# Attention, gated layer and soft mixture on one core: the token sum in feature halves, a second score bank, five raw buffers, and whole loads and stores at the end

## The chip, the cores and the metric

The kernel runs on one core of one Trainium2 chip. The metric is the device time of one execution, in microseconds (us). TensorE (PE) multiplies, VectorE (DVE), ScalarE (ACT) and GpSimd (POOL) work on elements, and SyncE (SP) issues every DMA of this kernel, in one queue and in program order.

## The reference

```python
scores = scale * np.matmul(q, k.transpose(0, 1, 3, 2))      # q, k, v: 4 x 12 heads x 448 x 64
scores = np.where(mask, -1e9, scores)                       # causal
attn = softmax(scores); x = (attn @ v) -> 1792 tokens x 768
h = x @ w_in                                                # 768 -> 2048, weights given as float64
g = h * clip(h + 3, 0, 6) / 6
x = g @ w_out                                               # 2048 -> 768, weights given as float64
logits = x @ phi                                            # 32 slots: 8 experts x 4
d = softmax(logits, over tokens);  slot_input = d.T @ x     # 32 x 768
h = maximum(slot_input[e] @ w1[e], 0); slot_out[e] = h @ w2[e]
c = softmax(logits, over slots);   return c @ slot_out      # 1792 x 768
```

The first gated layer is the bulk of the arithmetic. Since w_out is applied to all tokens only through phi and through the token sum d.T @ g, the kernel never forms g @ w_out: it forms w_out @ phi once, and U = d.T @ g (32 x 2048) with a running maximum over the four batches.

## The kernel before, in words

**Front.** Attention runs over 24 pairs of heads, six for each of four batches (function `attention`). A pair loads q, k, v, forms scores once for the row maxima (L476), takes the maxima on DVE (L491 or L495), forms the scores again transposed and in split float32r with the maximum subtracted (L526, L531), exponentiates (L541), multiplies with v (L564) and writes its columns of x (`xp`). Two PSUM banks as one tile `ps` hold scores; two single banks `t` hold transposes. Beside it `conv` turns the float64 weights into float32 (load into a `raw` buffer, of which there are three; ACT L627; DVE L630, L636, L639): 16 tiles of w_out first, then 16 tiles of w_in.

**The gated layer.** For each batch and each of 16 feature tiles `hmm` (L734) makes 18 matmuls of 128x448. ACT adds three and clips (`r`, L739), DVE multiplies (`g`, L741). In batch 0 w_in comes from `conv`; later batches reload it from DRAM (`wi_d`, into `cx`). Logits are gathered in one bank by L767.

**Sums of a batch.** The logits of the four column groups are added by one matmul (L809); DVE takes the maximum (L866, for the last batch L827), ACT the exponential. `ublocks` (L785) then makes 56 tiled matmuls into four banks. DVE adds the four banks into `U4`, four planes of 2048 values a partition's worth (L910, L857). After the last batch eight rounds fold `U` and `U4` (L1045, L1049, with the scale held in a buffer of pool `g`), copy to `wp` (L1054) and multiply with w_out (L1062) to the slot input.

**The mixture.** 64 loads of 768 KB bring w1 and w2 into ring buffers of 6 KB a partition. Memory for rings comes free in stages, since pools close one after the other: `cv_end`, `a_end`, `b_end`, `x_end` (after the last `cx`), `h_end` (after the last L734), `g_end` (pool of `g`, `r`, `ls`, `zT`), `m_end` (`gtok`), `o_end` (after the last L1062, five more buffers in w_out's place). `RINGS` tells how many buffers each gives: 1 at the start, then 4, 2, 3, 1, 6, 2, 3. Experts run in L1109 to L1133; then L1215 multiplies with w2. For the last two experts w2 comes in column halves, so that the chain to the outputs of columns 0 to 383 (L1230 to L1238, L1255, copies L1263/L1267, eight stores of 112 partitions) may run before the second half has landed.

**What sets the order.** `Schedule` is a list scheduler that runs while the program is built. Each step has a priority number (a due time from the table `TU`), a cost and its buffers; it is put on its engine when the planner's clock says that it can start. Where the planner sees PE idle, `filler` (L390) puts in 32x128 matmuls whose result is not used. What the engines then do is fixed, in that order.

## Time and profile before

| | us |
|---|---|
| median of 3 runs (654.37 to 656.09) | 655.76 |
| the profiled execution, its own time | 655.37 |
| its span, first to last instruction | 653.5 |
| PE busy in the span | 594.8 |
| DVE busy | 407.5 |
| ACT busy | 250.4 |
| POOL busy | 150.6 |

Fillers count as busy PE. Times in the rows are from the span's start. A chain of waits tells what released each piece of work; a table by windows tells how busy each engine was in a stretch, the granted clock of PE as a share of full speed (1.00 is 2.4 GHz, 0.50 is 1.2), the busy share of the 16 DMA engines and what they moved.

### The profile page before, as it was taken

The numbers are of one execution on the slowest core, as the hardware profiler recorded it, in microseconds if no ns is written. First come the engines' busy times: TensorE is split into PE (matmuls) and PEld (weight loads), VectorE is DVE, ScalarE is ACT, GpSimd is POOL, SyncE is SP. The second block draws the span as 40 slices with busy tenths as digits, with TensorE's granted clock in tenths as the row PEclk, the third lists the DMA queues.
The fourth block names the chain that finished last, engine by engine and source line by source line (L and its number), as shares of the span: only waits on it lengthen the run. The fifth ranks groups of instructions, "written<-read, shape, count | busy, mean of one in ns | idle before, by whom it ended". The sixth has DMA issues, their size and how long they took to land.

```text
span 653.5 us, 14639 instructions
## 1 busy us (share of the span) xinstructions
PE 594.8 (91%) x5816; PEld 446.1 (68%) x5816; DVE 407.5 (62%) x948; ACT 250.4 (38%) x420; POOL 150.6 (23%) x212
## 2 busy tenths in 40 slices
PE   7799899988988889999999999999999999998582
PEld 5688676766877678758878777888788654463021
DVE  6889888679886796787686867555655423010032
ACT  2466556445455554524344541433333201110032
POOL 1234446424462222323234322210000010000000
PEclk8899999899998999999999999999999999879877
DMA  7998878879879789872676543279833449999987
GB/s 205 314 294 254 217 213 207 189 168 241 171 199 252 171 194 249 219 168 76 121 164 125 135 91 79 73 206 402 314 97 97 174 175 416 415 414 414 393 291 252
DMA packets 196244, 144.59 MB, mean 221 GB/s; under 512 B 154704, under 2 KB 174672, under 8 KB 196176
## 3 DMA queue, kind: packets, MB, share of 16 engines
q1 hardware_dynamic: 196176, 143.66, 74.5%
q8 instruction: 46, 0.75, 0.5%
q14 instruction: 22, 0.18, 0.1%
HBM read 121.41 MB, written 22.22 MB: 220 GB/s over the span
## 4 chain that ended last, share of the span: by engine, by line
PE 45%; DMA 12%; DVE 10%; SPq 2%; ACT 2%; issue 2%; DVEq 0%; ACTq 0%
PE ph L734 25%; DMA ring<-in_moe_w_dram 8%; DMA raw<-in_moe_w_in_dram 3%; DVE ps L491 3%; PE ps L526 2%; SPq L406 2%; PE t L1124 2%; PE o L564 2%; PE pl L767 1%; PE t L785 1%; PE ps L1109 1%; PE pl L734 1%; PE ph L1109 1%; PE ps L476 1%; PE o L1062 1%
## 5 line engine op out<-in xcount | busy, mean ns | idle before, releaser
L734 PE MATMUL ph<-xp,wpl 128*128 128x448 f32 x1098 | 238.3, 372 | 2.4 <-DVE wpl L723 2.3
L734 PEld LDWEIGHTS ph<-xp,wpl 128*128 128x128 f32 x1098 | 204.0, 189 | 32.7 <-issue 8.7
L739 ACT ACTIVATE r<-ph,three 128x448 f32<-128x448 f32 x61 | 38.6, 632 | 124.0 <-PE ph L734 119.3
L549 POOL TENSOR_SCALAR_AFFINE_SELECT s<-s 128x256 f32<-128x256 f32 x96 | 49.6, 540 | 145.4 <-ACT s L541 140.1
L741 DVE SCALAR_TENSOR_TENSOR g<-r,ph 128x448 f32<-128x448 f32 x61 | 37.5, 614 | 55.4 <-ACT r L739 52.4
L491 DVE CUSTOM_DVE_ANT_0 ps<-ps,maskw 128x448 f32<-128x448 f32 (+3 forms) x144 | 61.7, 428 | 15.1 <-PE ps L476 10.5
L725 POOL TENSOR_TENSOR wpl<-cx,wpl 128x768 fp32r<-128x768 f32 x26 | 49.8, 1916 | 80.7 <-ACT wpl L720 74.8
L720 ACT ACTIVATE wpl<-cx 128x768 fp32r<-128x768 f32 x64 | 53.6, 838 | 29.6 <-PE ph L734 16.0
L526 PE MATMUL ps<-qp,kp 64*64 64x64 f32 (+3 forms) x576 | 58.2, 309 | 6.7 <-DVE mc L491 2.7
L541 ACT ACTIVATE s<-ps 128x896 f32<-128x896 f32 (+2 forms) x72 | 50.0, 731 | 28.6 <-PE ps L531 25.8
L526 PEld LDWEIGHTS ps<-qp,kp 64*128 64x128 f32 (+1 forms) x576 | 42.4, 177 | 22.5 <-ACT s L541 5.1
L564 PE MATMUL o<-vr,s 128*64 128x65 f32 (+1 forms) x1536 | 53.6, 224 | 0.0
L564 PEld LDWEIGHTS o<-vr,s 128*64 128x64 f32 (+1 forms) x1536 | 48.6, 137 | 5.0 <-issue 2.9
L627 ACT ACTIVATE ca<-raw 128x768 f32<-128x768 f32 x32 | 29.4, 919 | 46.8 <-DMA raw<-in_moe_w_in_dram 26.3
L723 DVE TENSOR_TENSOR wpl<-cx,wpl 128x768 fp32r<-128x768 f32 x38 | 35.8, 943 | 3.9 <-ACT wpl L720 3.6
L476 PE MATMUL ps<-kp,qp 64*128 64x448 f32 (+1 forms) x192 | 27.3, 342 | 11.5 <-DVE mc L495 4.0
L745 DVE STREAM_TRANSPOSE gtok<-g 128x448 f32<-128x448 f32 x48 | 29.7, 632 | 4.0 <-PE ps L785 3.1
L636 DVE SCALAR_TENSOR_TENSOR cw<-ca,cw 128x768 uint32<-128x768 uint32 x32 | 30.7, 958 | 2.2 <-ACT ca L627 0.7
L476 PEld LDWEIGHTS ps<-kp,qp 64*128 64x128 f32 x192 | 14.4, 173 | 23.9 <-issue 10.1
L630 DVE TENSOR_SCALAR cw<-raw 128x768 uint32<-128x768 uint32 x30 | 18.7, 622 | 19.0 <-DMA raw<-in_moe_w_in_dram 11.1
L531 PE MATMUL ps<-dg,oner 64*128 64x448 f32 (+1 forms) x192 | 28.4, 295 | 0.0
L1215 PE MATMUL o<-ring,wos 128*32 128x384 f32 x108 | 21.3, 627 | 5.7 <-DMA ring<-in_moe_w_dram 5.7
(236 smaller groups left out, 802.0 us busy)
## 6 DMA issues: line engine op xcount, KB each, us to landing
ring<-in_moe_w_dram SPq DMA_DIRECT2D x54, 768.0 KB, 14.6
cx<-wi_d SPq DMA_DIRECT2D x48, 384.0 KB, 3.5
raw<-in_moe_w_out_dram SPq DMA_DIRECT2D x16, 768.0 KB, 6.4
raw<-in_moe_w_in_dram SPq DMA_DIRECT2D x16, 768.0 KB, 6.9
wos<-in_moe_w_dram SPq DMA_DIRECT2D x10, 768.0 KB, 15.1
wo_d<-gtok SPq DMA_DIRECT2D x16, 384.0 KB, 3.5
wi_d<-cx SPq DMA_DIRECT2D x16, 384.0 KB, 3.8
wos<-wo_d SPq DMA_DIRECT2D x16, 384.0 KB, 5.9
```

Source lines behind the costliest of these rows:

```text
L476: nc.tensor.matmul(ps.t[:n, h, c:c + w], pl["q"].t[r, 0, q0:q0 + n], pl["k"].t[r, 0, 0:w], start=(t == part[0][0]), stop=adds, skip_group_ ...
L491: nc.vector.tensor_tensor_reduce(out=x, in0=x, in1=maskw[:n, 320 - q0:320 + n] if t else maskw[:n, 320:320 + n], scale=-1.0, scalar=3.0e38 ...
L526: nc.tensor.matmul(ps.t[:kn, h, col:col + n], pl["k"].t[r, x, q0:q0 + kn], pl["q"].t[r, y, q0:S], start=(c == 0 and col == 0), stop=False, ...
L541: nc.scalar.activation(out=o, in_=x, func=ACTF.Exp, scale=SCALE)
L549: nc.gpsimd.affine_select(out=x, in_=x, pattern=[[0, 2], [1, kn]], compare_op=ALU.is_ge, fill=0.0, base=0, channel_multiplier=-1)
L564: nc.tensor.matmul(o.t[64 * h:64 * h + 64, VD * j:VD * j + VD], s.t[:kn, h, c:c + 64], vr.t[:kn, h, t, :], start=(t == 0), stop=(t == ts[- ...
L720: e = sc.add("ACT", 0.84, lambda w=w, cx=cx: nc.scalar.activation(out=w.t[:, 0], in_=cx.t, func=ACTF.Copy), [cr], [cx, w], ps_)
L723: ("DVE", 1.0, lambda w=w, cx=cx: nc.vector.tensor_sub(w.t[:, 1], cx.t, w.t[:, 0].bitcast(F32))),
L725: ("POOL", 2.0, lambda w=w, cx=cx: nc.gpsimd.tensor_sub(w.t[:, 1], cx.t, w.t[:, 0].bitcast(F32))),
L734: nc.tensor.matmul(h.t[:, :S], w.t[:, a, kk, :], x.t[:, c, kk, :], start=(n == 0), stop=(n == len(seq) - 1))
L739: rr = sc.add("ACT", 0.63, lambda h=h, r=r: nc.scalar.activation(out=r.t, in_=h.t[:, :S], func=ACTF.Relu, bias=three), [hh], [h, r], pr - ...
L741: gg = sc.add("DVE", 0.62, lambda h=h, r=r, g=g: nc.vector.scalar_tensor_tensor(out=g.t, in0=r.t, scalar=6.0, in1=h.t[:, :S], op0=ALU.min, ...
```

## The change

It has four visible parts and a new order. (1) `U4` is gone: `collect` copies the four banks of `ublocks` to SBUF (in `gtok`'s memory), adds them with four column-tiled matmuls and folds them into one `U`; after the last batch this is done in two halves of eight feature tiles, `U` is turned by DVE into `wp`, and w_out is multiplied from there without the eight rounds. `U` of batch 0 is brought into the same layout by four transposes. `r` is gone (ACT writes into `g`, DVE multiplies in place). Logits go to tokens by four DVE block transposes straight from the bank (`logits_out`), without ACT copy and PE transposes. (2) When the last user of `t` is done, its two banks become a second `ps` tile. (3) Five `raw` buffers instead of three; rings now come as 0, 6, 2, 4, 1, 5, 2, 3. (4) All w2 loads are whole; after the last one both column halves are finished, and outputs are stored by seven stores of 128 partitions, with 14 tokens of the output to a partition and two of them (6 KB) in a store. (5) The table and the planner's costs are other numbers, and the planner adds a cost where PE changes between full-array and tiled matmuls (`TURN`, `KEEP`).

```diff
-TU = {'PO': [-130.96, ...], ..., 'RINGS': [1, 4, 2, 3, 1, 6, 2, 3], ..., 'RAW': 3, ...}
+TU = {'KEEP': 2.63, 'PO': [-133.04, ...], ..., 'RINGS': [0, 6, 2, 4, 1, 5, 2, 3], ..., 'RAW': 5, ...}
...
-    U4 = const.tile([P, KF, 4, 32], F32, name="U4")
...
-        many(mog, TU["R"], "r", [P, S])
...
-        ptt = many(pst, 2, "t", [P, 512])
+        ptt = pst.tile([P, 2, 512], F32, name="pt")
+        sc.pool("t", [ptt[:, 0], ptt[:, 1]])
...
+            def collect(banks, bufs, um, up, c0, n, deps, pr, v0=0):
+                part = gflat[:, c0:c0 + 4 * n].rearrange("p (i x) -> p i x", i=4)
+                ev = []
+                for i in range(4):
+                    ev.append(sc.any([
+                        ("ACT", 0.16 + n * 0.84e-3, lambda i=i: nc.scalar.activation(
+                            out=part[:, i], in_=banks()[i][:, :n], func=ACTF.Copy)),
+                        ("DVE", 0.1 + n * 1.04e-3, lambda i=i: nc.vector.tensor_copy(part[:, i], banks()[i][:, :n])),
+                    ], [um], bufs, pr))
+
+                def total():
+                    for i in range(4):
+                        nc.tensor.matmul(
+                            up()[32 * i:32 * i + 32, :n], sel4[:, 0, :], part[:, i],
+                            start=True, stop=True, tile_position=(0, 32 * i))
+
+                m = sc.add("PE", 0.2 + n * 1.7e-3, total, ev, bufs, pr)
+                return sc.add("DVE", 0.1 + n * 1.04e-3, lambda: nc.vector.scalar_tensor_tensor(
+                    out=U[:, v0:v0 + n], in0=U[:, v0:v0 + n], scalar=c1(SAL), in1=up()[:, :n],
+                    op0=ALU.mult, op1=ALU.add), [m] + deps, bufs, pr), ev
...
+            def logits_out(lr, deps, pr, b=b):
+                def turn():
+                    for i in range(4):
+                        r = slice(32 * i, 32 * i + 32)
+                        n = (S // 32 - i + 3) // 4
+                        nc.vector.transpose(
+                            ltok[r, b, 0:n], lr.t[r].rearrange("p (t i x) -> p t i x", i=4, x=32)[:, 0:n, i])
...
-                    u_part.append(sc.add("DVE", 1.4, uadd, [um, sal, s0, prev_u], ub + [u2], T1 + hf))
+                    um = sc.add("PE", 2.2, lambda hf=hf, banks=banks: ublocks(banks(), zT, 8 * hf, 8),
+                                [zd] + lasts, [gtb, zT] + bufs, T1 + 3 * hf)
+                    u, ev = collect(banks, [gtb] + bufs, um, lambda banks=banks: banks()[0], hf * DFF * 7 // 4, 256,
+                                    [sal, prev_u], T1 + 3 * hf + 1, 256 * hf)
+                    u_part.append(sc.add("DVE", 0.38, lambda hf=hf: nc.vector.transpose(
+                        wp[:, 8 * hf:8 * hf + 8, :].rearrange("p f s -> p (f s)"), U[:, 256 * hf:256 * hf + 256]),
+                        [u], [], T1 + 3 * hf + 1))
...
+        def t_end():
+            sc.free["t"].clear()
+            sc.grant("ps", ptt)
...
-        ge = sc.add("SP", 0.0, g_end, [he] + sc.users("g", "r", "ls"), [], 0)
+        ge = sc.add("SP", 0.0, g_end, [he] + sc.users("g", "zT", "ls"), [], 0)
...
-        for ci in range(2):
-            for e in range(SPLIT, E):
-                for k0 in (0, 4):
-                    l = w2load(e, k0, 4, ci, 1, ci)
...
+        for e in range(E):
             for k0 in range(0, 8, 2):
-                l = w2load(e, k0, 2, 0, 2, 0)
+                w2load(e, k0)
...
+        rows = out.rearrange("(p t) d -> p t d", t=TR)
+        for t0 in range(0, TR, 2):
+            ob, ev = sc.buf("ring"), []
...
+            sc.load(0.76e6, lambda ob=ob, t0=t0: dma(rows[:, t0:t0 + 2], ob.t.rearrange("p (t d) -> p t d", t=2)),
+                    ev + [parts[-1][3]], [ob], T1 + 1200 + 10 * t0)
```

**PE, batch 0.** Between the third and the fourth group of 18 products of the gated layer (L734, in the changed kernel L740) the order before stands as follows; `g` are the gated tiles that are transposed, `qp`/`kp`/`dg` belong to an attention pair, and L390 is the filler.

```order
L751 MATMUL t_257<-ident,g_194 128x128 x3
L751 MATMUL t_257<-ident,g_194 64x128
L390 MATMUL ph_252<-ident 32x128 x4
L526 MATMUL ps_255<-qp_229,kp_231 128x448 x6
L531 MATMUL ps_255<-dg_239,oner 128x448 x2
L526 MATMUL ps_255<-qp_229,kp_231 64x64 x6
L531 MATMUL ps_255<-dg_239,oner 64x64 x2
L390 MATMUL ph_252<-ident 32x128 x3
L526 MATMUL ps_255<-qp_229,kp_231 128x320 x6
```

In the changed kernel the same engine has, from the third group on:

```order
L740 MATMUL ph_248<-xp_194,wpl_197 128x448 x18
L532 MATMUL ps_251<-qp_222,kp_224 128x320 x6
L537 MATMUL ps_251<-dg_232,oner 128x320 x2
L532 MATMUL ps_251<-qp_222,kp_224 128x192 x6
L537 MATMUL ps_251<-dg_232,oner 128x192 x2
L758 MATMUL pt<-ident,g_189 128x128 x3
L758 MATMUL pt<-ident,g_189 64x128
```

No filler stands there any more. Counted over the whole order: before the 16th and last group of batch 0 stand the products with v of 15 attention pairs before and of 12 now, and fillers are 46 ahead of the first group and 28 from there to the 16th before, 37 and none now. From the 40th group on the two orders hold the same work.

**PE, after the last batch.** `zT` is the transposed exponential, `U` the sums, `sel` a selection matrix; L1062 (now L1061) is the product with w_out. Before:

```order
L785 MATMUL ps_255<-gtok,zT_199 32x512 x2
L390 MATMUL o_256<-ident 32x128 x5
L1045 MATMUL ph_253<-g_196,U 128x64
L1049 MATMUL ph_253<-sel_74,U_82 128x32 x2
L1045 MATMUL pl<-g_196,U 128x64
L1049 MATMUL pl<-sel_74,U_82 128x32 x2
L1045 MATMUL ph_252<-g_196,U 128x64
L1049 MATMUL ph_252<-sel_74,U_82 128x32 x2
L1062 MATMUL o_256<-wos,wp 32x384 x4
```

Now:

```order
L789 MATMUL o_252<-gtok,zT_193 32x256
L807 MATMUL ps_251<-gtok,sel_74 32x256 x4
L807 MATMUL ph_249<-gtok,sel_74 32x256 x4
L1061 MATMUL pt<-wos,wp 32x384 x32
L394 MATMUL pt<-ident 32x128
L1078 MATMUL pt<-selb,wos 128x64 x3
```

The eight rounds are gone, and with them the last reader of a `g` buffer (`g_196`).

**SP, the first loads of the mixture.** Each `ring` row is one load of 768 KB, in the order in which SP issues them around the end of the gated layer. Before, ten ring loads stand ahead of these rows:

```order
L406 DMA cx_205<-wi_d_190 128x768
L406 DMA ring_5676<-in_moe_w_dram 128x1536
L406 DMA ring_5708<-in_moe_w_dram 128x1536
...
L406 DMA ring_5728<-in_moe_w_dram 128x1536
L406 DMA ring_5826<-in_moe_w_dram 128x1536
L406 DMA ring_5830<-in_moe_w_dram 128x1536
L406 DMA ring_5856<-in_moe_w_dram 128x1536
```

Now twelve stand ahead:

```order
L411 DMA cx_199<-wi_d_185 128x768
L411 DMA ring_5656<-in_moe_w_dram 128x1536
L411 DMA ring_5688<-in_moe_w_dram 128x1536
...
L411 DMA ring_5704<-in_moe_w_dram 128x1536
L411 DMA ring_5865<-in_moe_w_dram 128x1536
L411 DMA ring_5869<-in_moe_w_dram 128x1536
L411 DMA ring_5906<-in_moe_w_dram 128x1536
```

ring_5676/ring_5656 take `x_end`'s place, the next six (now five) `h_end`'s, ring_5826 and ring_5830 (now 5865 and 5869) `g_end`'s, the next three `m_end`'s; five loads into w_out's place follow in both.

## Rows read from the trace of the kernel before

**Rows 1.** The page's span in 40 equal slices, in tenths.

```profile
PEclk8899999899998999999999999999999999879877
DMA  7998878879879789872676543279833449999987
```

**Rows 2.** Windows: start:end length, busy of PE, PEld, DVE, ACT, POOL, PEclk, DMA share, GB/s.

```profile
0.00:250.00 250.00, 223.29 (x2681) 180.49 (x2682) 203.54 (x452) 129.46 (x217) 94.09 (x144) 0.96 0.84 219
250.00:516.00 266.00, 263.23 (x2187) 214.63 (x2187) 174.94 (x405) 101.00 (x161) 54.70 (x67) 1.00 0.59 160
516.00:520.00 4.00, 3.54 (x30) 1.53 (x29) 2.09 (x5) 1.17 (x2) 0.00 (x0) 1.00 0.68 223
520.00:525.00 5.00, 4.05 (x113) 2.26 (x115) 1.70 (x9) 1.09 (x4) 0.00 (x0) 1.00 1.02 419
525.00:530.00 5.00, 4.88 (x50) 3.33 (x36) 3.71 (x11) 0.00 (x0) 0.00 (x0) 1.00 0.85 346
530.00:535.00 5.00, 5.00 (x47) 2.78 (x43) 0.68 (x3) 0.00 (x0) 1.50 (x1) 1.00 0.02 7
535.00:540.00 5.00, 4.42 (x44) 2.24 (x44) 0.94 (x4) 0.10 (x1) 0.31 (x1) 1.00 0.41 107
...
575.00:610.00 35.00, 29.24 (x337) 13.32 (x336) 3.50 (x10) 3.37 (x6) 0.00 (x0) 0.85 1.02 415
610.00:620.00 10.00, 5.31 (x40) 0.88 (x40) 0.00 (x0) 0.00 (x0) 0.00 (x0) 0.76 1.04 381
620.00:625.00 5.00, 3.54 (x20) 0.40 (x16) 0.20 (x1) 0.00 (x0) 0.00 (x0) 0.50 1.07 373
625.00:630.00 5.00, 4.46 (x20) 1.26 (x21) 0.97 (x2) 0.49 (x1) 0.00 (x0) 0.61 0.95 333
...
640.00:645.00 5.00, 1.56 (x6) 0.89 (x6) 1.63 (x4) 1.94 (x5) 0.00 (x0) 1.00 1.03 325
```

**Rows 3.** Windows of the fillers alone (L390): length, busy of PE, PEld.

```profile
0.00:100.00 100.00, 17.39 (x96) 10.69 (x96) 0.93 0.84 247
100.00:250.00 150.00, 9.81 (x66) 6.15 (x66) 0.98 0.84 200
```

**Rows 4.** The page's costliest groups: busy, mean ns of one, idle before and its releaser.

```profile
L491 DVE CUSTOM_DVE_ANT_0 ps<-ps,maskw 128x448 f32<-128x448 f32 (+3 forms) x144 | 61.7, 428 | 15.1 <-PE ps L476 10.5
...
L526 PE MATMUL ps<-qp,kp 64*64 64x64 f32 (+3 forms) x576 | 58.2, 309 | 6.7 <-DVE mc L491 2.7
...
L564 PE MATMUL o<-vr,s 128*64 128x65 f32 (+1 forms) x1536 | 53.6, 224 | 0.0
...
L627 ACT ACTIVATE ca<-raw 128x768 f32<-128x768 f32 x32 | 29.4, 919 | 46.8 <-DMA raw<-in_moe_w_in_dram 26.3
...
L476 PE MATMUL ps<-kp,qp 64*128 64x448 f32 (+1 forms) x192 | 27.3, 342 | 11.5 <-DVE mc L495 4.0
...
L630 DVE TENSOR_SCALAR cw<-raw 128x768 uint32<-128x768 uint32 x30 | 18.7, 622 | 19.0 <-DMA raw<-in_moe_w_in_dram 11.1
L531 PE MATMUL ps<-dg,oner 64*128 64x448 f32 (+1 forms) x192 | 28.4, 295 | 0.0
```

**Rows 5.** Timeline of DVE at the last batch's maximum: start, us, idle before.

```profile
519.14 0.63 DVE L827 TENSOR_REDUCE st<-t 128x1 f32<-128x448 f32 x1 [1.02 <-ACT r L823]
```

**Rows 6.** The chain that ended last, sums and slot input: start, us, what.

```profile
525.84 1.65 DVE U L857 x4
...
537.35 2.14 PE o L1062 x24
```

**Rows 7.** Waits of SP's DMA queue: us in total, times, longest.

```profile
SPq L406 <- PE pl L1045: 15.1, 1, 15.1
```

**Rows 8.** The chain that ended last, from the last useful load on.

```profile
625.33 1.51 PE ph L1215 x8
626.84 1.59 PE t L1233 x2
...
631.75 3.56 DMA out_dram<-ring
```

More of the change, by code (lines that the diff above doesn't have):

```diff
@@ L846 @@
[L846 to L861 removed]
+                ldone = logits_out(lr, [la], T1 + 2)
@@ new lines, with banks @@
+                ua, ub = [sc.buf("ps") for _ in range(2)], [sc.buf("h") for _ in range(3)] + [sc.buf("o")]
+                u_part = []
+                for hf, bufs in enumerate((ua, ub)):
+                    def banks(hf=hf):
+                        return [u.t for u in ub] if hf else [u.t[:, x] for u in ua for x in range(2)]
+                    um = sc.add("PE", 2.2, lambda hf=hf, banks=banks: ublocks(banks(), zT, 8 * hf, 8),
[5 more added lines that the diff above has]
+                        [u], [], T1 + 3 * hf + 1))
+                    if not hf:
+                        si, si_free = ua[1], ev
@@ L883 @@
             if b:
[L884 to L886 removed]
+                logits_out(lr, [a], pr + 1)
             zz = sc.add("ACT", 0.9 if b else 1.2, exz, [a], [lr, z], pr)
@@ new lines, with simm @@
+        for m in range(KF // 2):
+            def simm(m=m):
+                for d in range(2):
+                    for r in range(2):
+                        g = d * 2 + r
+                        nc.tensor.matmul(
+                            si.t[32 * g:32 * g + 32, 0, :384], wp[:, 2 * m + r, :],
+                            held["wo"][:, 2 * m + r, d * 384:(d + 1) * 384],
+                            start=(m == 0), stop=(m == KF // 2 - 1), tile_position=(0, 32 * g),
+                        )
+            smm = sc.add("PE", 0.73, simm, [u_part[m // 4]] + (si_free if not m else [smm]) + wol, [si], T1 + 4 + m)
@@ new lines, in w2load, with ymm @@
+            parts.append((e, k0, w, sc.load(0.76e6, ld, [], [w], T1 + 1000 + e)))
+        for e in range(E):
+            for k0 in range(0, 8, 2):
+                w2load(e, k0)
+        accs, ylast = [sc.buf("acc0"), sc.buf("acc1")], None
+        def ymm(e, k0, w):
+            for k in range(2):
+                for c in range(2):
+                    j = (k0 + k + 2 * c) % 4
+                    nc.tensor.matmul(
+                        accs[c].t[32 * j:32 * j + 32, :384], held["hT"][:, e, k0 + k, :],
+                        w.t[:, k * DM + c * 384:k * DM + c * 384 + 384],
+                        start=(e == 0 and k0 < 4), stop=(e == E - 1 and k0 > 3), tile_position=(0, 32 * j),
+                    )
@@ new lines, with oev @@
+        rows = out.rearrange("(p t) d -> p t d", t=TR)
+        for t0 in range(0, TR, 2):
+            ob, ev = sc.buf("ring"), []
+            for c in range(2):
+                for t in range(2):
+                    op = sc.buf("q")
+                    pr = T1 + 1200 + 10 * t0 + c
+                    m = sc.add("PE", 0.17, lambda op=op, c=c, t=t0 + t: nc.tensor.matmul(
+                        op.t[:, :384], held["cT"][:, t], sl[c](), start=True, stop=True), [done[c]] + cplane, [op], pr)
+                    def oev(copy, op=op, ob=ob, at_=t * DM + c * 384):
+                        copy(ob.t[:, at_:at_ + 384], op.t[:, :384])
```

280 lines of the change are left out of this document (98 added, 182 removed).

## The prediction, made before the result

> **What bounds the kernel now.** I read the page's slices first [rows 1]: the granted clock is near full in the first 34 of 40 slices, so clock is no topic there, and the DMA digits fall to 3, 3, 4, 4 in slices 30 to 33 ahead of a run at 9. Slices 30 and 31 (474 to 507 us) lie under a PE that is full; slice 33 (523 to 539) doesn't. Then the windows [rows 2] give three stretches.
>
> From 0 to 250 us nothing alone is the bound: PE 223.3 busy, DVE 203.5, DMA share 0.84. But of PE's time there 17.4 + 9.8 = 27.2 us are fillers [rows 3] and 250 - 223.3 = 26.7 us are idle, so 54 us pass without useful work on PE. From 250 to 516 PE works 263.2 of 266 us: it is the bound, and whatever waste the front avoids moves the 516 earlier one for one.
>
> After the last product (516) DMA sets the end. It moves 223, 419 and 346 GB/s to 530, then 7 and 107 GB/s to 540, then 415 GB/s until the column halves begin, which run at 381, 373 and 333 GB/s [rows 2]. The hole has one cause: SP waits 15.1 us, once, for L1045 on PE [rows 7], the last reader of pool `g`, before it may load into `g_end`'s rings; and L1045 is in the eight rounds that run from the U adds at 525.84 to 537.35 + 2.14 = 539.5 [rows 6]. Behind the last loads stands the chain from 625.33 to the first store's issue at 631.75, and the stores at 325 GB/s [rows 2, 8]. The span ends at 653.5; the profiled run took 655.37, so 1.9 us lie around the span, and the median of the three runs is 0.4 above it.
>
> **Tail, part by part.** *Ring gap.* Between 516 and 540 DMA moves 4 x 223 + 5 x (419 + 346 + 7 + 107) = 5.3 MB [rows 2]. With rings free it would have moved from 518 on 22 x 0.415 = 9.1 MB. The difference, 3.8 MB, is 9.2 us at 415 GB/s. In the changed order the last reader of a `g` buffer is gone from the rounds and `g_end` hangs on `zT`, free once the last `ublocks` end at some 526; the six rings before that last until about 529. SP may still wait a little there: I take 1.5 us, and gain 7.7 (bounds 0, if another wait holds the same rings, and 9.2).
>
> *Two loads fewer.* Twelve instead of ten ring loads stand ahead of the last `cx` load; two loads of 0.786 MB at 415 GB/s leave the DMA-bound stretch: 3.8 us. They go where DMA's share is 0.59 and PE the bound, so their cover is 40% of free DMA time.
>
> *Whole w2.* The loads landed from 610 to 630 moved 10 x 381 + 5 x 373 + 5 x 333 = 7.34 MB, which takes 17.7 us at 415: 2.3 us gained (0 if the last window's 333 was the ramp-down alone and returns: then 1).
>
> So the last load would land some 13.8 us sooner, at 616 if the 516 stood still.
>
> *End chain.* Before, the first half's chain runs under the second half's loads: DMA is still at 0.95 up to 630 [rows 2], and the first store is issued at 631.75, 1.75 us after. Now both halves follow the last load. The same chain takes 631.75 - 625.33 = 6.4 us from its first product [rows 8], and the other half's products (1.51) come on top: 7.9, which is 6.2 more. Part of rows 8 ran at half clock (0.50 and 0.61 in 620 to 630, rows 2), and new fillers stand there now; if they keep the clock full, L1233's 1.59 becomes 0.8. I take that, and lose 5.4. Bounds 3 (the products halve too, and the second half's evictions overlap the first's) and 8.
>
> *Stores.* 5.5 MB at 325 GB/s are 17.0 us. Rows of 6 KB instead of 1.5 KB: loads show 415 against 377 for the same two sizes, so I scale 325 to 358 GB/s: 15.4, a gain of 1.6 (bounds 0 and 3).
>
> By the Trainium skill (DMA: Bandwidth & Descriptors, Specifications) a transfer reaches line rate from 512 B on; by this both 1.5 KB terms would be nothing, and the sum 3.9 us smaller. The rows speak against it for the loads (381 and 373 against 415 GB/s); no row shows stores in 6 KB rows.
>
> *Sums and slot input.* The rounds become 64 products of L1062 without waits: 24 of them take 2.14 [rows 6], so 64 take 5.7, half of them before the second half's sums are there. Against that stand evictions, the block sum (512 columns; L1233's 1.59 for two at about half clock [rows 8] gives 0.8 to 1.1) and a fold. The four U adds, 1.65 us of the chain [rows 6], vanish. The slot input comes some 5 us sooner, near 534. Since the experts then run under the loads until 580 or so, this is worth nothing at the end beyond what the rings and w_out's memory already have in the sum.
>
> *The logits.* Before, DVE's maximum waited 1.02 us for ACT's read of the same bank [rows 5]: two reads, and yet in turn. The changed order puts four DVE transposes on that bank ahead of the exponential, so ACT waits for them, by about as much as that 1.02, while the copy by ACT is saved; PE has nothing queued that this path would free, and DMA has six rings to fill meanwhile. I put it at 0.
>
> The Trainium skill (PSUM — Partial Sum Buffer, PSUM bank collisions raise a hardware error) says that instructions of different engines on one bank and quadrant are ordered, reads among them; the 1.02 us agrees. It speaks against `logits_out` and against sharing evictions of one bank between ACT and DVE, by some 0.5 to 1 us on the way to the slot input.
>
> Tail in sum: 7.7 + 3.8 + 2.3 - 5.4 + 1.6 = **10.0 us** gained (all worst ends: 0 + 3.8 + 1 - 8 + 0 = -3; all best: 9.2 + 3.8 + 2.3 - 3 + 3 = 15).
>
> **Front.** An attention pair costs PE (58.2 + 28.4 + 53.6 + 27.3) / 24 = 7.0 us [rows 4]. Three pairs fewer stand ahead of the 16th product group, so that group must come 21 us sooner for PE only to break even: what is not done before it has to be done in the saturated stretch. PE also gets about 3 us more work, an estimate: two block sums of 512 columns (each about twice the 0.8 that one product of L1233 takes, less for the clock, rows 8) and four transposes of `U` for batch 0, less those that brought logits to tokens. So the front changes the time by 21 + 3 - e, with e the lead of the 16th group.
>
> e from supply: counting SP's order, the last raw load stands behind 48.4 MB instead of 50.7 MB; 2.3 MB at 219 GB/s [rows 2] are 10.5 us. With five buffers the waits for raw tiles shrink too: DVE L630 stood idle 19.0 us, mostly for them, ACT L627 46.8 [rows 4]; ACT has slack, DVE less, so 10.5 + 19.0 = 29.5 is the upper end. Four L630 (0.62 us each, rows 4) go to ACT and six diagonals to POOL, off a DVE that is 81% busy, and three pairs' maxima, some 6 x 0.43 us a pair [rows 4], come later as well.
>
> e from PE: 74 fillers cost 27.2 us [rows 3] or 0.37 each. Ahead of the first group nine are gone (3.3 us) and behind it all 28 (10.3). Does PE then idle there instead, e is 21 + 3 = 24; does it not, e is 21 + 13.6 = 35. The two accounts overlap between 24 and 29.5. I take 26: the front gains 26 - 24 = **2 us**. Ends: e = 10.5 loses 13.5, e = 35 gains 11; half of the whole 54 us of waste saved would be 27 - 3 = 24.
>
> **Sum:** 655.4 - 10.0 - 2 = 643.4 for the profiled run's kind, and with the median 0.4 above, 643 to 644; I write 643.
>
> **Rivals.**
> *Front gains much.* The 54 us without useful work [rows 2, 3] halve, since neither raw buffers nor PSUM banks hold PE up: 655.4 - 10 - 24 = 621. For it: no fillers between the first group and the 16th, and the idle is spread over waits for DVE (15.1 us before L491, 6.7 before L526, 11.5 before L476, rows 4). Against it: DVE at 81% and DMA at 84% leave little room for both.
>
> *Ring gap stays.* The rings of `g_end` wait for another late reader, evictions in `gtok` or the transposes; 7 GB/s shows again, 7.7 us are lost: 651. Against it: `zT` is read last by `ublocks`.
>
> *Slower: w_in comes no sooner.* If the raw loads are held by DMA's own 0.84 and not by buffers, e is about 0 to 10.5, three pairs' work is moved behind the 16th group, and PE waits there: 655.4 - 10 + 13.5 = 659 with e = 10.5, 669 with e = 0. It decides below e = 24 - 10 = 14 us. For it: both bytes and DVE work ahead of that group are nearly the same. Against it: the waits of L627 and L630 are ended by raw loads, and loads wait for buffers.
>
> *It doesn't do what it says.* Half a clock in the front: without fillers PE's granted clock falls as in 620 to 630 [rows 2]. It stays at 0.96 with 26.7 us idle there, so I leave it inside the slower case.
>
> **How the numbers follow.** Forecast 0.58 (634 to 650 by the ends above, 643 likeliest); front gains much 0.15 (621 to 633); ring gap stays 0.13 (647 to 654); w_in no sooner 0.14 (656 to 669). The range 626 to 653 leaves out the slower case and part of the first rival, about 2 in 10. A measurement of this kernel tells 0.3% (2 us) from no change: faster 0.82, same 0.06, slower 0.12.
>
> **What would show it.** In the changed kernel's windows: no stretch of 5 us under 300 GB/s between some 518 and the last load; SP's list without a wait of over 5 us for PE ahead of `g_end`'s rings; fillers plus idle of PE in the first 250 us near 50, and the last product at about 514; the last load near 614, the first store's issue 7 to 8 us later, stores near 358 GB/s. A last product behind 516 makes the front step wrong, a hole in DMA the ring step, and a delay of over 9 us or a clock of 0.50 behind the last load the end chain.

## The result, and the profile after

The changed kernel takes 635.7 us (633.66 to 639.2, four runs) against 655.9 for the kernel before on the same chip; the ratio is 0.969 with a 95% interval of 0.963 to 0.975. A second series (`after_again`, below) gave 637.7 against 657.7, ratio 0.969 (0.965 to 0.973). Forecast were 643 and a range of 626 to 653: sign and range hold, but the gain is 20 us where 12 were forecast. What doesn't hold is how the gain is made up: some 10 of the tail and 2 of the front were forecast, and the two profiled executions show 8.2 and 13.4.

The profiled execution took 633.66 us, its span is 631.9. The last product group ends at 502.7 instead of 516.1, and from there to the end it is 129.2 us instead of 137.4. The page's slices, to be read beside [rows 1]:

```profile
PEclk7899998899999799999999999999999988897998
DMA  7999788889987796666766756947233379999938
```

The windows, with the columns of [rows 2]. Two differences matter most: PE is busier in the first 250 us, and the hole in DMA, a stretch in which little is loaded, is still there, shorter, around 515 to 520 (98 GB/s).

```profile
0.00:250.00 250.00, 230.14 (x2550) 188.06 (x2552) 199.18 (x415) 136.62 (x230) 105.93 (x154) 0.93 0.86 238
250.00:495.00 245.00, 241.44 (x2225) 197.15 (x2222) 172.40 (x406) 96.13 (x153) 53.09 (x87) 1.00 0.60 158
...
510.00:515.00 5.00, 4.89 (x171) 4.08 (x152) 0.95 (x3) 0.66 (x2) 0.00 (x0) 0.68 0.79 325
515.00:520.00 5.00, 3.29 (x36) 1.33 (x40) 2.39 (x6) 0.66 (x2) 0.00 (x0) 1.00 0.38 98
520.00:525.00 5.00, 4.09 (x53) 1.44 (x45) 0.75 (x3) 0.33 (x1) 1.81 (x1) 1.00 1.01 417
...
605.00:610.00 5.00, 3.67 (x35) 1.98 (x31) 0.56 (x1) 0.49 (x1) 0.00 (x0) 1.00 0.24 98
...
620.00:625.00 5.00, 2.53 (x12) 1.60 (x10) 3.06 (x6) 2.49 (x6) 0.00 (x0) 1.00 1.01 414
```

The fillers alone (now L394), as in [rows 3]:

```profile
0.00:100.00 100.00, 15.79 (x84) 9.72 (x84) 0.90 0.87 263
100.00:250.00 150.00, 0.62 (x4) 0.36 (x4) 0.95 0.86 221
```

In the first 250 us PE spends 16.4 us on fillers and idles 19.9: 36.3 us without useful work, where [rows 2, 3] gave 54. That is 17.6 us less, and the last product comes 13.4 us sooner.

The wait that answers to [rows 7] has another reader at its end. SP now waits for the last `ublocks`:

```profile
SPq L411 <- PE o L789: 8.4, 1, 8.4
```

And the chain that ended last, from the last load on, beside [rows 8]:

```profile
608.18 0.51 PE o L1207
609.10 0.55 DVE wos L1228
609.78 1.54 PE pt L1230 x4
...
614.51 0.50 ACT ring L1251
615.03 0.57 DVE ring L1248
```

### The profile page after: what moved, and what is told of

It reads as the page before. It is cut to its first block, busy times and chain, and to the rows that moved or that the text cites. A ratio compares the mean times of both kernels' runs of the same rounds, so it can differ in the third digit from the quotient of the medians.

```text
span 631.9 us, 14691 instructions
## 1 busy us (share of the span) xinstructions
PE 580.3 (92%) x5844; PEld 445.1 (70%) x5844; DVE 403.4 (64%) x908; ACT 253.4 (40%) x426; POOL 160.8 (25%) x242
## 4 chain that ended last, share of the span: by engine, by line
PE 46%; DMA 14%; DVE 3%; ACT 2%; issue 1%; SPq 1%; POOL 0%; DVEq 0%; ACTq 0%
PE ph L740 20%; DMA ring<-in_moe_w_dram 9%; PE pl L740 8%; PE o L570 4%; DMA wos<-in_moe_w_dram 2%; PE ps L532 2%; DMA cx<-wi_d 1%; PE pt L532 1%; PE ps L789 1%; DMA xt<-xd 1%; PE ph L774 1%; PE pt L1061 1%; PE ps L482 1%; SPq L411 1%; PE ps L1244 1%
## 5 line engine op out<-in xcount | busy, mean ns | idle before, releaser
L740 PE MATMUL ph<-xp,wpl 128*128 128x448 f32 x846 | 185.5, 374 | 1.6 <-POOL wpl L731 1.6
L740 PEld LDWEIGHTS ph<-xp,wpl 128*128 128x128 f32 x846 | 157.6, 190 | 27.1 <-ACT g L746 5.9
L746 ACT ACTIVATE g<-ph,three 128x448 f32<-128x448 f32 x47 | 29.8, 635 | 107.3 <-PE ph L740 107.2
L740 PE MATMUL pl<-xp,wpl 128*128 128x448 f32 x306 | 66.7, 371 | 0.0
L748 DVE SCALAR_TENSOR_TENSOR g<-g,ph 128x448 f32<-128x448 f32 x47 | 28.9, 615 | 55.4 <-ACT g L746 55.4
L740 PEld LDWEIGHTS pl<-xp,wpl 128*128 128x128 f32 x306 | 56.7, 188 | 7.1 <-issue 1.8
L497 DVE CUSTOM_DVE_ANT_0 ps<-ps,maskw 128x448 f32<-128x448 f32 (+3 forms) x108 | 46.2, 427 | 8.6 <-PE ps L482 3.7
L532 PE MATMUL ps<-qp,kp 64*128 64x448 f32 (+2 forms) x468 | 47.6, 311 | 2.0 <-DVE rc L582 1.9
L547 ACT ACTIVATE s<-ps 128x896 f32<-128x896 f32 (+2 forms) x62 | 41.0, 702 | 20.7 <-PE ps L537 20.5
L532 PEld LDWEIGHTS ps<-qp,kp 64*128 64x128 f32 (+1 forms) x468 | 34.6, 176 | 14.3 <-issue 5.0
L482 PE MATMUL ps<-kp,qp 64*128 64x448 f32 (+3 forms) x156 | 23.3, 353 | 10.2 <-ACT s L547 3.7
## 6 DMA issues: line engine op xcount, KB each, us to landing
wos<-in_moe_w_dram SPq DMA_DIRECT2D x10, 768.0 KB, 15.1
```

Source lines behind the costliest of these rows:

```text
L497: nc.vector.tensor_tensor_reduce(out=x, in0=x, in1=maskw[:n, 320 - q0:320 + n] if t else maskw[:n, 320:320 + n], scale=-1.0, scalar=3.0e38 ...
L532: nc.tensor.matmul(ps.t[:kn, h, col:col + n], pl["k"].t[r, x, q0:q0 + kn], pl["q"].t[r, y, q0:S], start=(c == 0 and col == 0), stop=False, ...
L547: nc.scalar.activation(out=o, in_=x, func=ACTF.Exp, scale=SCALE)
L740: nc.tensor.matmul(h.t[:, :S], w.t[:, a, kk, :], x.t[:, c, kk, :], start=(n == 0), stop=(n == len(seq) - 1))
L746: rr = sc.add("ACT", 0.63, lambda h=h, g=g: nc.scalar.activation(out=g.t, in_=h.t[:, :S], func=ACTF.Relu, bias=three), [hh], [h, g], pr - ...
```

## The experiments

Where the time is meant, each kernel is compared with the kernel before on the same chip, and where the place is meant, by its trace. Since executions of one order differ by several us in the front (last section), the stretch from the start of the 64th and last product group to the end of the span is the measure for edits of the tail: 141.3 us before (512.2 to 653.5), 133.2 after (498.7 to 631.9; 133.3 in `after_again`). Within it the landing of the last load divides what comes ahead of it from what comes behind. From the last product to that landing the executions whose tail differs only behind it lie between 104.9 and 105.5 us, so half a us there is scatter.

### The front: five buffers, the second bank, the order

**a_raw3**, three float64 buffers, two rings more at the start:

```diff
-'RINGS': [0, 6, 2, 4, 1, 5, 2, 3], ... 'RAW': 5
+'RINGS': [2, 4, 2, 4, 1, 5, 2, 3], ... 'RAW': 3
```

> The changed kernel with three float64 buffers instead of five; the two buffers become rings that are free from the start, so that the number of loads ahead of the last w_in tile stays 12. The planner writes its order anew. Theory (the front gained 13 us because conversions no longer wait for a buffer): the 16th group of products goes back from 221 us to about 240 or later, fillers plus idle of PE in the first 250 us from 36 to 48 or more, and the time is 646 to 652. Rival (the second score bank and the order did it): 634 to 641, and the waste stays under 42. The tail from the last product on stays at 129 us by both.

Measured: 653.6 us, ratio to the kernel before 0.997 (0.993 to 1.001). The 16th group starts at 235.9 us, between the 248.9 of before and the 220.9 of after. In 0 to 235.9 fillers take 18.5 us and PE idles 28.1. The first row below is the window, the second the fillers in it:

```profile
0.00:235.90 235.90, 207.82 (x2411) 167.74 (x2411) 188.80 (x381) 124.69 (x206) 100.00 (x156) 0.93 0.84 226
...
0.00:235.90 235.90, 18.48 (x100) 11.89 (x100) 0.93 0.84 226
```

The direction is the theory's, 15 us of lead are lost, but the time is worse than it said: the stretch from the 16th to the 64th group is 7 us longer too (284.8 against 277.8), and the 64th group starts at 520.6, later than the 512.2 of the kernel before.

**a_nobank**, without the second double bank; the four sums of a batch go into `ps` and the two `t`:

```diff
-        sc.add("SP", 0.0, t_end, sc.users("t"), [], 0)
...
-                ub = [sc.buf("ps") for _ in range(2)]
+                ub = [sc.buf("ps"), sc.buf("t"), sc.buf("t")]
```

> The changed kernel without the second score bank: the two banks of t stay apart, the four sums of a batch go into ps and the two t, as in the kernel before. The rest is unchanged, the planner writes the order behind the last user of t anew. Theory (the buffers did the front): 634 to 640, the 16th group within 3 us of 221. Rival (the bank did it): 644 to 652, with PE idle ahead of L482 or L532 again above 15 us in the first 250.

Measured: 659.4 us, ratio to before 1.003 (0.999 to 1.007). The 16th group starts at 222.1, so the lead of 27 us over the kernel before stays whole without the bank, and more than the gain is lost behind it: from the 16th to the 64th group it takes 304.1 us, and the 64th starts at 526.2. Windows of that stretch, all work and fillers alone, then the same stretch of the changed kernel, which has no filler there:

```profile
222.10:526.20 304.10, 292.43 (x2585) 235.26 (x2583) 190.97 (x451) 113.15 (x183) 68.80 (x103) 0.99 0.56 151
...
222.10:526.20 304.10, 14.76 (x108) 10.58 (x108) 0.99 0.56 151
...
220.90:498.70 277.80, 274.15 (x2478) 223.67 (x2475) 189.95 (x450) 112.83 (x183) 64.83 (x104) 1.00 0.62 165
```

Fillers (14.8) and idle PE (11.7) make 26.5 us there, against 3.7 in the changed kernel. Each theory was half right: the lead doesn't need the bank, but without it the stretch behind the 16th group, into which attention pairs were moved, has holes. A lead that isn't followed by a full stretch is given back.

**a_oldtab**, the numbers of the kernel before in the table, the structure of the changed one:

```diff
-TU = {'KEEP': 2.63, 'PO': [-133.04, -17.63, -10.01, -36.65], ...
+TU = {'KEEP': 0.0, 'PO': [-130.96, -7.26, -2.82, -5.86], ...
```

> The changed kernel with the numbers of the kernel before in the planner's table (due times, biases, look-ahead), no cost for a turn in the choice of a step; buffers, banks and rings stay those of the change. Theory (memory for five buffers and a second score bank make the front's gain, the table only follows): 640 or less, the 16th group before 230 us. Rival (the order written by the new numbers makes it): 648 to 656.

Measured: 658.4 us, ratio to before 1.001 (0.999 to 1.003). The 16th group starts at 247.1, fillers and idle PE are 27.1 + 28.8 us in the first 250. The 64th group starts at 525.1. With the old numbers the new memory and bank bring the front nothing. So with any one of the three, buffers, bank and numbers, taken away the front's gain is gone. How the 13 us divide among them these runs can't say. The planner wrote a new order each time, with numbers that fit another structure, and each of the three starts its 64th group 22 to 28 us behind the changed kernel and 8 to 14 behind the kernel before: a part that is taken away costs more than all three bring together. No run adds one part alone to the kernel before. The tail keeps its gain in all three (132.0 to 132.9 us from the 64th group to the end).

### The tail: the ring gap

**b_scale**, the kernel before with `U` scaled in place, so that no round reads a `g` buffer:

```diff
-tensor_scalar_mul(idS.t[:, 0:P], ident, c1(SAL0)), [s0], [idS], T1 + 1)
+tensor_scalar_mul(U, U, c1(SAL0)), [s0, prev_u], [], T1 + 1)
...
-up.t[:, :64], U[:, c * P:(c + 1) * P], idS.t[:, 32 * j0:32 * j0 + 64],
+up.t[:, :64], U[:, c * P:(c + 1) * P], ident[:, 32 * j0:32 * j0 + 64],
```

> The kernel before, where the first U is multiplied by its scale in place and the products of L1045 take the identity from constants, so that the pool of g has no reader in the eight rounds. Theory (the hole of 530 to 540 is that one wait): SP issues the two loads behind the last ublocks, near 526.5, no stretch of 5 us between 520 and 600 shows under 300 GB/s, and the time falls by 6 to 8 us to 648 to 650. Rival (another wait holds the same rings): the hole stays and the time is 655 to 656.

Measured: 645.9 us, ratio 0.985 (0.977 to 0.994). From the 64th group to the end 135.0 us, 6.3 less than before. SP's 15.1 us for L1045 have become 4.4 for the last `ublocks`, and the hole is gone:

```profile
SPq L406 <- PE ps L785: 4.4, 1, 4.4
```

```profile
530.00:535.00 5.00, 4.88 (x47) 3.61 (x44) 3.38 (x11) 0.00 (x0) 0.00 (x0) 1.00 1.01 410
535.00:540.00 5.00, 5.00 (x50) 2.71 (x42) 0.68 (x3) 0.00 (x0) 1.80 (x1) 1.00 1.01 403
```

(the stretch before lay 3.6 us later in this execution). One wait on one buffer held the rings, and taking the reader away, alone, is worth 6.3 us by the trace. The last load lands 107.0 us behind the last product instead of 115.4, which is 8.4 sooner; 2 of these are lost again behind it, in the chain (1.1 us to the first store's issue instead of 0.2) and the stores (22.9 instead of 21.75).

**a_gearly**, the `g` buffers in a pool that closes behind the last logits, so that loads may start there ahead of the last `ublocks`; every engine's order stays:

```diff
+        def gg_end():
+            mgg.close()
+            rings(1)
...
-        ge = sc.add("SP", 0.0, g_end, [he] + sc.users("g", "zT", "ls"), [], 0)
+        gge = sc.add("SP", 0.0, gg_end, [he] + sc.users("g"), [], 0)
+        ge = sc.add("SP", 0.0, g_end, [gge] + sc.users("zT", "ls"), [], 0)
```

> The changed kernel with the g buffers in a pool of their own, closed behind the last logits (some 505 us) instead of behind the last ublocks (517): one more 768 KB load may start there. Every engine's order is that of the changed kernel. Theory (what is left of the hole of 513 to 519 us is that wait, and every load that fits into it counts): the time falls by 1.9 us, one load at 415 GB/s. Rival (the loads behind are held by something later): no change. The front is the same by both, so the stretch from the last product on is compared: 133.2 us from the 64th group's start to the end, 131.3 by the theory.

Measured: 634.7 us, and 133.0 us from the 64th group to the end against 133.2. The rival holds. By the trace two loads, not one, start early (508.1 and 508.7), and the hole only moves. Its windows, and then the wait of SP ahead of the next load:

```profile
515.00:520.00 5.00, 3.36 (x123) 2.28 (x101) 1.18 (x3) 0.66 (x2) 0.00 (x0) 0.94 1.02 416
520.00:525.00 5.00, 4.68 (x58) 1.98 (x60) 2.16 (x5) 0.66 (x2) 1.62 (x1) 1.00 0.61 189
```

```profile
SPq L412 <- PE ph L808: 12.4, 1, 12.4
```

No memory is added by it, so what could be loaded is only loaded earlier, and SP then waits for the next stage of memory. L808 (L807 in the changed kernel) are the block sums of the second half: they read `gtok`, in whose place the next three loads go. These start at 521.6, the five into w_out's place at 524.65, with waits of 0.9 us at most. So behind the last `ublocks` it is the sums that hold the rings, and the slot input itself hardly.

**a_expfirst**, the four transposes of the last logits behind the exponential:

```diff
-                ldone = logits_out(lr, [la], T1 + 2)
+                ldone = logits_out(lr, [la, zz], T1 + 2)
```

> The changed kernel with the four transposes of the last batch's logits behind the exponential instead of ahead of it; only two DVE instructions change their place. In the changed kernel ACT's exponential starts at 507.23 behind these transposes though the maximum is ready at 506.0, PE idles 3.6 us ahead of the last ublocks, and these run at a granted clock of 0.68 in 510 to 515 and take 8.1 us, where the kernel before idled 2.4 us, kept 1.00 and took 4.3. Theory A (the wait for the shared bank costs itself and the clock): ublocks start 1.2 us sooner after the last product, keep the clock, and end 4 us sooner; w_out's memory is released 4 us sooner, the hole in DMA shrinks from 5 us to about 1, and the time falls by 3 to 4 us; from the 64th group's start to the end 129 to 130 instead of 133.2. Theory B (the wait alone): 1.2 us less, 132. Rival (nothing of the slot input reaches the end): 133.

In the changed kernel the maximum is ready at 506.0 and ACT's exponential starts at 507.23, when DVE has read the bank (start, us, what, and the idle time before with its releaser):

```profile
505.92 1.21 DVE L821 STREAM_TRANSPOSE ltok<-pl 32x128 f32<-32x128 f32 x4
```

```profile
507.23 0.63 ACT L851 ACTIVATE ls<-pl,st 128x448 f32<-128x448 f32 x1 [3.89 <-DVE ltok L821]
```

Measured: 636.0 us beside 637.7 for `after_again` (ratios to the same runs of before 0.9666 and 0.9691, intervals overlap); from the 64th group to the end 132.2 us, against 133.2 and 133.3 in the two traces of the changed kernel. Theory B is nearest: the wait costs about 1 us and that is all that comes back, by the trace; the times don't tell it from nothing. The first half's `ublocks` do keep the clock and take 2.6 us instead of 3.6. But behind them PE now waits 2.8 us for nothing that the trace shows ("issue"), and the clock is at 0.50 a little later, under the second half and the products with w_out (7.2 us instead of 5.4). First the changed kernel's group, then two rows of this one's chain of waits, then its windows:

```profile
L789 PE MATMUL ps<-gtok,zT 32*32 32x256 f32 x56 | 3.6, 506 | 2.3 <-DVE zT L859 2.3
```

```profile
512.73 2.83 issue
...
518.77 7.20 PE pt L1061 x64
```

```profile
513.50:515.50 2.00, 0.00 (x0) 0.00 (x0) 0.00 (x0) 0.00 (x0) 0.00 (x0) 1.00 0.44 172
515.50:517.50 2.00, 1.94 (x17) 0.75 (x20) 0.42 (x1) 0.66 (x2) 0.00 (x0) 0.52 0.00 0
517.50:519.50 2.00, 1.72 (x20) 0.40 (x18) 1.67 (x4) 0.00 (x0) 0.00 (x0) 0.50 0.92 261
```

### The tail: whole loads, chain and stores

**a_oldend**, the changed kernel with the w2 loads, chain and stores of the kernel before (the whole block from the w2 loads to the end is exchanged).

> The changed kernel with the end of the kernel before: w2 of the last two experts in column halves, eight stores of 112 partitions. By the sum of the prediction (whole w2 +2.3, stores +1.6, end chain -5.4) the old end is 1.5 us better: 634. Rival (the new chain is no longer than the old one, since from the last load to the end both kernels take some 23.6 us, and only the loads are faster): 638, 2 us worse. Both leave everything ahead of 590 us as it is.

Measured: 637.6 us, ratio to before 0.971 (0.963 to 0.979), not to be told from the changed kernel by its times; from the 64th group to the end 134.3 us against 133.2. So by the trace the new end is 1.1 us better, where the sum had it 1.5 worse. The trace divides it: the last load lands 106.9 us behind the last product instead of 105.5 (whole loads gain 1.4), the first store is issued 1.2 us behind it instead of 7.5 (the chain loses 6.3), and from there to the end it is 22.2 us instead of 16.3 (the stores gain 5.9).

**a_q4**, the outputs go through banks of four tiles instead of three:

```diff
-            for t in (pth[1], ptl[0], pts[0][:, 0], pts[0][:, 1]):
+            for t in (pth[1], ptl[0], pts[0][:, 0], ptt[:, 0]):
```

> The changed kernel with the four banks into which the outputs go taken from four tiles instead of three: two halves of one tile make ACT's and DVE's copies run in turn (ACT 615.00, then DVE, then the next products). Theory (the stores are paced by these copies, 1.79 us per store of two tokens): the pace falls to 1.1 to 1.3 us, the last store is issued 3 to 4 us earlier and the end comes 2 us sooner, where DMA's rate takes over. Rival (the stores are at DMA's own rate of some 337 GB/s): no change at the end.

Measured: 635.2 us; from the 64th group to the end 131.5, 1.7 less than 133.2. Issues of the seven stores, first start and total, and the time from issue to landing, of the changed kernel and of this one, and this one's DMA beside it:

```profile
615.62 11.08 SPq L411 DMA_DIRECT2D out_dram<-ring  x7
...
DMA to landing us min/median/max: 3.3/3.6/4.4
```

```profile
619.33 7.62 SPq L411 DMA_DIRECT2D out_dram<-ring  x7
...
DMA to landing us min/median/max: 3.3/6.0/8.6
```

```profile
620.00:625.00 5.00, 4.97 (x19) 2.88 (x18) 4.71 (x10) 4.48 (x11) 0.00 (x0) 1.00 1.00 404
```

Seven issues follow each other at 1.1 us instead of 1.8, as the theory said: in the changed kernel ACT and DVE copied two halves of one tile in turn. But the end doesn't follow. From the first store's issue to the end of the span it is 16.3 us in both, the later stores only wait longer to land, and DMA stores at 404 GB/s here and at 414 in the changed kernel (620 to 625 above). So for the stores the rival holds, at a higher rate than it named. What the edit gains is the first store, which needs four such copies: it is issued 6.4 us behind the last load's landing instead of 7.5. That is 1.1 of the 1.7 us; the other 0.6 lie ahead of that landing, where nothing was changed.

**a_nofill_end**, no fillers beside the last expert's loads (the step `fill_on` is left out):

> The changed kernel without the fillers that run beside the last expert's w2 loads. Theory (they keep the clock full for the end chain): the granted clock falls to 0.5 in the last 10 us of the loads as in the kernel before, the chain from the last load to the first store grows from 7.4 to 9 or 10 us, 2 us more in time. Rival (the clock recovers under the products of the chain itself): under 0.7 us more.

Measured: 637.3 us, 134.5 from the 64th group to the end (+1.3). The clock falls at the last loads and again under the outputs:

```profile
605.00:611.00 6.00, 4.57 (x28) 0.66 (x32) 0.00 (x0) 0.00 (x0) 0.00 (x0) 0.53 0.66 269
...
620.00:636.00 16.00, 7.60 (x18) 5.06 (x18) 5.52 (x11) 4.18 (x10) 0.00 (x0) 0.50 0.80 321
```

The theory named the wrong place. From the last load (610.95) to the first store (618.26) it is 7.3 us, as with fillers (7.4); the store issues then stretch from 11.1 to 13.4 us, under output products at half clock, and the stores take 18.2 us to the end instead of 16.3.

**a_q4g** and **a_best** combine edits: four tiles with the early pool, and four tiles with the exponential ahead.

> Both edits, the early pool and the four tiles. If each is worth what its theory says they add up, since one lies before the loads and one behind them: 3.9 us less, 129.3 us from the start of the 64th group to the end. If the loads hide one of them: 2 us less.

Measured: 634.5 us and 131.8, which is 1.4 less than the changed kernel: the four tiles' gain and nothing for the pool, in keeping with `a_gearly`.

> Both edits that the traces give a price to: outputs copied from four tiles (the end 1.7 us sooner by its trace) and transposes of logits behind the exponential. By theory A 128 us from the 64th group's start to the end and 630 to 631 in all, by B 130 and 632.

Measured: 633.2 us (632.2 to 635.3), ratio to before 0.9635 (0.961 to 0.966), and 130.4 from the 64th group to the end, 2.8 less: 1.1 behind the last load's landing, as in `a_q4`, and 1.7 ahead of it. It is the shortest tail of all. Against the changed kernel on the same chip (0.9691, 0.965 to 0.973) the time is some 0.6% less, with intervals that just touch.

**after_again**:

> The changed kernel once more, on the same chip as the other runs of this call, so that they can be compared with it and not with a run of another day: 634 to 637, 133 us from the 64th group's start to the end, and a DMA hole of about 5 us ahead of 520 whose length doesn't depend on the run.

Measured: 637.7 us (633.5 to 640.6), 133.3 from the 64th group to the end, and the hole again.

## Why the prediction held, and which steps did not

**What bounds the kernel.** The three stretches were read rightly: 250 to the last product is still PE's (241.4 of 245 up to 495), and a lead in the front arrives there, less the work that was moved behind it.

**Front, the term that was mis-sized.** Its form, 21 + 3 - e, had the right idea, and e was good: the 16th group starts 28.0 us sooner, 26 were taken. The rival that w_in comes no sooner fails: the last `raw` load lands at 200.3 instead of 232.0, and ACT's and DVE's waits for these loads fall from 53 us (34.6 and 18.6) to 24 (17.5 and 6.5). Wrong were the 24. Work behind the 16th group grew far less, as PE's busy time between that group's start and the last product shows, after and before:

```profile
220.90:502.70 281.80, 278.15 (x2496) 227.33 (x2494) 191.55 (x452) 112.83 (x183) 64.83 (x104) 1.00 0.62 165
```

```profile
248.90:516.10 267.20, 264.43 (x2194) 215.76 (x2192) 176.01 (x408) 101.77 (x163) 54.70 (x67) 1.00 0.59 161
```

The stretch grew by 281.8 - 267.2 = 14.6, so 28.0 - 14.6 = 13.4 us were won. Two reasons. First, the price of a pair, 7.0 us, was a sum of four lines' busy times [rows 4], and these lines lie on each other in time; the rows show them on parts of the array (`64*128`, `128*64`). The same lines in the window 248.9 to 516.1 of the kernel before:

```profile
L526 PE MATMUL ps<-qp,kp 64*128 64x448 f32 (+3 forms) x216 | 21.2, 302 | 0.9 <-DVE mc L491 0.7
L564 PE MATMUL o<-vr,s 128*64 128x65 f32 (+1 forms) x576 | 20.1, 224 | 0.0
...
L531 PE MATMUL ps<-dg,oner 64*128 64x448 f32 (+3 forms) x72 | 10.4, 288 | 0.0
...
L476 PE MATMUL ps<-kp,qp 64*128 64x448 f32 (+3 forms) x64 | 8.2, 333 | 1.6 <-DVE rc L576 1.3
```

They add up to 59.9 us for nine pairs. All PE groups of that window add up to 290.6, and PE was busy 264.4: 26 us are counted twice, there and in `ublocks`. The time in which PE had nothing but these four lines to do is 46.9 us, or 5.2 a pair; in the changed kernel's window above it is 59.6. These 12.7 us are nearly all of PE's 13.7 us of growth. Second, a pair isn't moved whole: between 16th group and last product the products with v rose from 9 pairs to 12, the transposed scores (L526, now L532) from 216 to 276 products, two and a half pairs. The extra 3 us were part of the 24; of them the trace shows 2.1 in this window, the 16 products of the block sums (L807).

So the front's 12 to 13 us lie just beyond the 11 that the account by fillers gave as its upper end, and the rival that the front gains much (24) came half way true.

**Ring gap.** The place and its cause were right, and `b_scale` shows them alone: 8.4 us at the last load's landing, near the 9.2 of the hole, and 6.3 at the end. The 1.5 us that were allowed for a new wait were too little. From 510 to 520 DMA moves some 2 MB less than at 415 GB/s, 4.9 us, and the gain is 9.2 - 4.9 = 4.3 instead of 7.7. The last `ublocks` end at 517.0, 14.3 us behind the last product, where in the kernel before it was 9.7 (516.1 to 525.8). Three things lie in between: exponential behind the transposes (1.2), a stall (1.5, last section) and half clock. The clock first, after and then before:

```profile
509.00:511.00 2.00, 2.00 (x100) 1.64 (x70) 0.37 (x2) 0.00 (x0) 0.00 (x0) 0.69 1.01 421
511.00:513.00 2.00, 2.00 (x71) 1.82 (x51) 0.73 (x2) 0.21 (x1) 0.00 (x0) 0.50 1.01 418
```

```profile
521.00:523.00 2.00, 1.49 (x49) 0.82 (x65) 1.24 (x6) 0.15 (x1) 0.00 (x0) 1.00 1.01 421
523.00:525.00 2.00, 2.00 (x74) 1.16 (x47) 0.00 (x0) 0.00 (x0) 0.00 (x0) 1.00 1.01 418
```

**Logits.** The wait of ACT for DVE's reads came as described, 1.2 us where "about 1.02" stood. The Trainium skill (PSUM — Partial Sum Buffer, PSUM bank collisions raise a hardware error) has the rule that instructions of two engines on one bank and quadrant are made to depend on each other, reads too, and the 507.23 above agrees with it. Putting it at 0 was wrong: `a_expfirst` gives back 1.0.

**Slot input.** Its products ended at 524.1, that is 21.4 us behind the last product instead of 23.4, 2 us sooner where 5 were expected. That it is worth nothing beyond the rings isn't refuted; what was left out is that the sums ahead of it read `gtok`, and `a_gearly` shows that this read is the next to hold the rings (12.4 us). The rival "ring gap stays" had named readers of `gtok`.

**Two loads fewer** (3.8) was not run alone, but the traces count it: 51 loads land behind the last product instead of 53, at 1.89 us each where nothing holds them. **Whole w2** (2.3) measured 1.6: the last eight loads take 15.1 us to land instead of 16.8, and 16.7 in `a_oldend`. With the ring gap's 4.3 they make 9.7.

The last load lands 105.5 us behind the last product (608.1 after 502.7). For the kernel before the prediction took 630 from the edge of a window; its last load, issued at 619.66, landed at 631.5, which is 115.4 us behind the last product:

```profile
L406 SPq DMA_DIRECT2D ring<-in_moe_w_dram x1: 1951/1951/1951, 619.7 to 619.7; - x1
...
DMA to landing us min/median/max: 11.8/11.8/11.8
```

So it comes 9.9 us sooner, and the three terms explain it, where 13.8 were forecast.

**End chain.** 7.4 us from the last load's product to the first store's issue; 7.9 less 0.8 were expected. That length is right, also that the fillers keep the clock there (1.00 in 605 to 610). The loss was mis-sized by the same misread landing: in the kernel before the first store is issued 0.2 us behind it (631.75) and not 1.75, so the chain loses 7.2 and not 5.4.

**Stores.** This term was mis-sized by 3.9: from the first store's issue to the end it is 631.9 - 615.6 = 16.3 us against 653.5 - 631.75 = 21.75 before, 5.5 gained and not 1.6. The step took the stores before for DMA-bound at 325 GB/s all the way, by one window of 5 us; 5.5 MB at that rate are 17.0 us, and nearly 5 more passed. And the new stores don't run at 358 GB/s but at 414 and then 392 (620 to 630), with DMA's share at 1.01 and 0.97; `a_q4` shows that a faster pace of copies doesn't shorten them. With the chain's loss of 7.2 the end as a whole loses 1.8 us, against 3.8 in the sum.

By the Trainium skill (DMA: Bandwidth & Descriptors, Specifications) rows of 1.5 KB should already have had the full rate. Stores in such rows moved 325 GB/s at a share of 1.03 [rows 2], those in rows of 6 KB 414 at 1.01; but they also had 112 partitions instead of 128, so the row's size is not alone in this. The column-half loads of `a_oldend`, at 373 GB/s beside 416 for whole ones in the same execution, speak against it once more.

**Sum.** Tail 8.2 for 10.0 (9.9 - 7.2 + 5.5), front 13.4 for 2. That the tail came out near its forecast is luck in part: too much for the loads (3.9) and the chain (1.8) and too little for the stores (3.9) partly cancel. The front's error is the rest, and the range was wide enough for it. The signs to look for told this: a hole under 300 GB/s was there, fillers plus idle were 36 and not 50, the last product came at 502.7 and not at 514.

## What to carry to other kernels

When work is moved across a point, price it by PE's busy time in a window that holds it less that of a window that doesn't, not by adding lines that share the array. A hole in the load queue has as many causes as there are stages of memory behind it: taking one wait away shows the next. A faster pace of issues is worth nothing where the queue behind them is full: look at landings, not at issues. And when buffers, PSUM and order are planned together, taking one away under numbers that fit all three (22 to 28 us lost for a gain of 13) says that the plan needs it, not what it is worth.

## What the runs showed of the hardware that was not expected

**One wait, two times.** The nine executions whose front has the changed kernel's order fall into two kinds. Behind the 16th group PE waits for DVE's maximum (L482), and right behind it L939 runs. In two of the nine that wait was 1.7 and 2.5 us, L939's 32 products took 0.60 us each (3.8 us), and it was 119 to 120 us from the 16th to the 32nd group. In the other seven it was 2.6 to 5.1 us, the products took 0.82 to 0.95 us each (5.4 to 6.3 us), and the stretch 122 to 125. The length of the wait alone doesn't part them (2.5 and 2.6 us), and why it differs no trace shows. First the changed kernel, then `after_again`, groups of PE in that stretch:

```profile
L482 PE MATMUL ps<-kp,qp 64*128 64x448 f32 (+3 forms) x40 | 5.0, 324 | 1.8 <-DVE mc L497 1.7
...
L939 PE MATMUL pt<-gtok,zT 128*32 128x512 f32 (+1 forms) x32 | 3.8, 597 | 0.0
```

```profile
L939 PE MATMUL pt<-gtok,zT 128*32 128x512 f32 (+1 forms) x32 | 6.3, 946 | 0.0
L482 PE MATMUL ps<-kp,qp 64*128 64x448 f32 (+3 forms) x40 | 5.3, 341 | 3.5 <-DVE mc L497 3.4
```

The same instructions in the same order so differ by up to 5 us, and part of the scatter of 633 to 640 us has its place here. The granted clock goes with it: 1.00 from 220.9 to 340.0 in the changed kernel, 0.97 from 220.7 to 344.0 in `a_q4`, whose wait was 3.4 us; it is 1.00 in both of the first kind and 0.97 to 0.99 in the seven. Over these nine executions the 64th group starts at 498.7 to 504.4, 501.9 on average, against 512.2 and 515.8 in the two traces with the order of before: the front's gain is some 12 us, which is also what the 20 us of both series leave behind the tail's 8, and the 13.4 of the profiled pair contains a lucky run.

**A stall without a releaser.** All nine, and `a_raw3` and `a_oldtab`, show PE standing 1.1 to 2.8 us within the last `ublocks`, with nothing that it waits for in the trace. The kernel before and `b_scale`, with 112 products there instead of 224, don't show it, nor does `a_nobank`, with 224. In the windows of `a_expfirst` above, the ring loads fill DMA when it begins and have run dry (0 GB/s) when it ends. The packets of DMA hold a likely cause: an execution of the changed kernel has 46 packets of 16 KB in an instruction queue (q8), and in all eleven one of them lands 1.3 to 1.6 us before PE goes on (in the changed kernel at 515.1, PE at 516.4). In `a_nobank` it lands at 542.5, behind the last `ublocks` (541.1). That PE stood for its instructions fits this; no run here varies it, and whether the loads held that packet up isn't shown.
